# The first batch's keys and queries as fp32 loads on SyncE, with TensorE transposes and a new order of work

## The chip, the cores and the metric

The kernel runs on one NeuronCore of a Trainium2 chip. Its engines each run their own instructions in order and wait for each other through semaphores: TensorE (PE; its loads of stationary operands are listed apart as PEld), VectorE (DVE), ScalarE (ACT), GpSimd (POOL) and SyncE (SP). Loads and stores are issued by POOL, SP or ACT into DMA queues. POOL's queue (software descriptors) can change the type on the way, here fp32 to bf16; SP's and ACT's queues move plain bytes or transpose. The metric is the device time of one execution in microseconds, the median of several runs.

## What is computed

An attention over pooled keys and values, whose output goes as x into a mixture of four causal attention heads ("experts"), of which each token takes the best two. Shapes: 8 batches, 8 heads, 576 tokens, 64 per head; 512 model columns; 4 experts of width 64.

```python
k_p = k.reshape(B, H, Sp, pool, D).mean(axis=3)          # pool = 8: 72 pooled keys
v_p = v.reshape(B, H, Sp, pool, D).mean(axis=3)
scores = scale * np.matmul(q, k_p.transpose(0, 1, 3, 2))
attn = softmax(scores);  attn_out = np.matmul(attn, v_p)
x = attn_out.transpose(0, 2, 1, 3).reshape(B, S, H * D)
...
logits = x @ w_gate;  topk = 2 largest;  w = softmax over them
for e in range(E):
    q, k, v = x @ wq[e], x @ wk[e], x @ wv[e]
    a = causal softmax(scale * q @ k.T)
    out += mask[e] * w[e] * (a @ v @ wo[e])
```

## The kernel before

One long string, `SEQ` (line 606), is the whole order of work. Each token is a step, `name:batch@bank`; a trailing `d` puts a copy on VectorE instead of ScalarE, a trailing `p` keeps a store from being issued right behind its copy. The loop at line 677 emits the tokens one after the other, and TensorE, ScalarE, VectorE and POOL run their instructions in exactly that order. The order was worked out beforehand by a planner; a change of plan is a change of this string. PSUM's eight banks are given out in it by number.

The steps of a batch, in order of their data flow:

- `L_q`, `L_k`, `L_v` (`load`, line 111): POOL loads queries, keys and values and casts them to bf16 into one of three buffers each (`qraws`, `kraws`, `vraws`). A key or value block has 96 partitions of two tokens each, for all heads; three blocks (c = 0, 1, 2) make 576 tokens.
- `PK` (line 249) pools keys: the stationary operand is the small matrix `poolk` (96x32), the moving one the keys. `kc` (line 258) transposes the pooled keys in blocks of 32 on VectorE, and `kt` (line 264) copies them to bf16 (`kpTs`). `u` (`turn`, line 277) transposes the queries on VectorE from `qraws` to `qTs`.
- `E` (line 293) makes scores, `e` (line 303) their exponentials on ScalarE into `etas`: per batch four activations of 1024 columns and two of 256. `D`, `d`, `x` make the denominators and their reciprocals (a logarithm and an exponential on ScalarE), `PV`, `vc` the pooled values, `O` the outputs, and `o` (VectorE) scales them into `xTs`.
- `P`, `p` project x to expert queries and keys, `V`, `v` to values and gate, `S`, `s` make causal scores and exponentials (`etbs`), `a` masks on POOL, `B` with `bz`, `bg`, `b` multiplies by the values, `T`, `t` (or `F`, a transposing DMA on SP) transposes, `Y`, `y` applies the output weights and `z` stores.
- `g` is the gate's arithmetic; `W`, `c` load and reorder the expert weights; `H` are warm-up matmuls on a zero operand, whose results nobody reads. `I`, `J`, `K`, `M` set constants and pads.

Batch 0 is treated apart. Its keys of heads 0 to 3 do not go through POOL: `Q0` to `Q2` (`load_plain`, line 130) load them as fp32 on SP into memory that `xTs[1]` uses later, in runs of 512 bytes, and `w0` to `w2` (`cast_plain`, line 134) cast them to bf16 on ScalarE. The other heads' keys (`L_k01`, `L_k11`, `L_k21`) and the queries come through POOL. `LONG` (line 59) gives batch 0's queries another layout: each partition reads 18 tokens in a row, in two loads of long runs. `PK`, `kc` and `kt` run in two halves for it, then `u0`, `u1`, `E0` and so on. The first eighteen warm-up matmuls (`H18`) stand ahead of all that. Batches 1 to 7 share one path.

The two lines that set batch 0's SyncE loads:

```python
nc.sync.dma_start(out=plain(c).rearrange("p (h n) -> p h n", h=4),
                  in_=k[0, 0:4, 2 * KR * c : 2 * KR * (c + 1), :].rearrange("h (p t) d -> p h (t d)", t=2))
```

## Time and profile before

| | before |
|---|---|
| median of 3 runs | 158.32 us (157.78 to 158.62) |
| the profiled execution | 159.01 us |
| its span, first to last instruction | 157.3 us |
| busy: TensorE, ScalarE, VectorE, POOL | 145.2, 136.0, 122.6, 88.5 us |
| granted TensorE clock, mean | 0.996 |
| DMA, POOL's queue / SP's and ACT's | 14.92 MB / 10.82 MB |

The rows of the profile are read like this. A row of the timeline has the start, the time until its last instruction ended, engine, line of the kernel, operation, output and input names, and a count of merged instructions; in square brackets how long the engine was idle before, and for whom it waited. A row of a group has the shape, the count, the busy time and the mean duration of one in nanoseconds, and after the second bar the idle time ahead of it. The chain of waits goes back from the last instruction to what released it, step by step, so what stands in it is what set the end. A row of stretches has the busy time of each engine, the number of its instructions in brackets, then the granted clock, the DMA share and GB/s. DMA rows count packets and bytes by queue: q0 is POOL's, q1 is SP's and ACT's. All times count from the start of the span.

### The profile page before, as it was taken

What the parts mean: (1) busy time and instruction counts of PE and PEld (TensorE: products, weight loads), DVE (VectorE), ACT (ScalarE), POOL (GpSimd) and SP (SyncE); (2) the same over time, 40 slices, a digit from 0 to 9 for tenths busy, and PEclk for the clock granted to TensorE, in tenths of its full rate; (3) what the DMA queues carried; (4) which work ended last, traced back from release to release, by engine and by line L of the source; (5) the groups of instructions that cost most, each with busy time, mean ns of one, the idle gap of its engine ahead of it and who ended that gap; (6) DMA issues with size and microseconds to landing.
All of it is one profiled execution on the core that took longest, in us unless ns stands there. A gap on an engine that the chain in (4) does not pass through costs nothing.

```text
span 157.3 us, 5462 instructions
## 1 busy us (share of the span) xinstructions
PE 145.2 (92%) x2133; PEld 80.1 (51%) x2133; DVE 122.6 (78%) x404; ACT 136.0 (86%) x256; POOL 88.5 (56%) x160
## 2 busy tenths in 40 slices
PE   6939789899999999999999999999999999999960
PEld 2313235445445547546645656466375666566620
DVE  1425285679899989989989999989869599888850
ACT  4123957999999999999999999999999999999850
POOL 6867557899896989892899233223200453323200
PEclk9999999999999999999999999999999999999998
DMA  4999999999999999999999992452330371499895
GB/s 109 163 187 180 181 178 151 179 166 178 182 182 181 179 181 180 181 215 247 181 179 180 213 108 42 44 167 77 100 70 8 105 236 26 120 303 382 258 375 160
DMA packets 68602, 26.47 MB, mean 168 GB/s; under 512 B 62304, under 2 KB 63712, under 8 KB 68576
## 3 DMA queue, kind: packets, MB, share of 16 engines
q0 software_dynamic: 57008, 14.92, 94.7%
q1 hardware_dynamic: 11344, 10.82, 22.3%
q10 hardware_dynamic: 224, 0.39, 0.7%
q8 instruction: 16, 0.26, 0.6%
q14 instruction: 10, 0.08, 0.2%
HBM read 30.42 MB, written 9.44 MB: 253 GB/s over the span
## 4 chain that ended last, share of the span: by engine, by line
PE 77%; DVE 6%; ACT 6%; DMA 5%; issue 2%; SPq 1%; DVEq 0%; ACTq 0%
PE psum L205 73%; DMA xT<-in_k_dram 5%; DVE xT L360 3%; ACT eta L314 2%; PE psum L214 2%; PE psum L193 2%; ACT etb L477 2%; DVE vaug L196 1%; ACT rza L333 1%; SPq L131 1%; DVE qT L281 0%; DVE xT L351 0%; ACT rza L337 0%; ACT kraw L196 0%; DVE kf L262 0%
## 5 line engine op out<-in xcount | busy, mean ns | idle before, releaser
L477 ACT ACTIVATE etb<-psum 128x1024 bf16<-128x1024 f32 x48 | 47.4, 1036 | 0.5 <-PE psum L205 0.4
L494 POOL TENSOR_SCALAR_AFFINE_SELECT etb<-etb 128x256 bf16<-128x256 bf16 x64 | 25.7, 413 | 27.1 <-ACT etb L477 26.7
L314 ACT ACTIVATE eta<-psum 96x1024 bf16<-96x1024 f32 (+1 forms) x48 | 36.3, 811 | 3.6 <-PE psum L205 3.0
L124 POOL DMA_DIRECT2D qraw<-in_q_dram x30 | 19.8, 662 | 4.6 <-DMA vraw<-in_v_dram 2.7
L205 PEld LDWEIGHTS <-etb 128*128 128x128 bf16 x480 | 18.3, 97 | 7.5 <-issue 2.0
L360 DVE TENSOR_TENSOR xT<-psum,rza 128x512 bf16<-128x512 f32 x32 | 20.4, 683 | 2.0 <-ACT rza L337 1.1
L124 POOL DMA_DIRECT2D vraw<-in_v_dram x24 | 18.5, 772 | 5.2 <-DMA vraw<-in_v_dram 1.9
L205 PE MATMUL psum<-wvg,xT 128*128 128x260 bf16 x144 | 20.5, 275 | 0.3 <-ACT eta L314 0.3
L205 PE MATMUL psum<-wop,oT 128*128 128x512 bf16 (+1 forms) x74 | 20.4, 375 | 0.4 <-DVE oT L196 0.4
L205 PE MATMUL psum<-xT,wqp 128*128 128x512 bf16 (+1 forms) x128 | 19.8, 287 | 0.5 <-DVE xT L360 0.4
L205 PE MATMUL psum<-vaug,etb 128*128 128x65 bf16 x480 | 20.2, 194 | 0.0
L205 PE MATMUL psum<-xT,wkp 128*128 128x512 bf16 (+1 forms) x128 | 19.6, 286 | 0.1
L124 POOL DMA_DIRECT2D kraw<-in_k_dram x24 | 18.2, 761 | 1.4 <-PE psum L205 0.4
L536 DVE TENSOR_TENSOR osc<-psum,gt 128x256 bf16<-128x256 f32 (+2 forms) x40 | 16.8, 423 | 1.2
L205 PE MATMUL psum<-qk 64*128 64x64 bf16 (+4 forms) x192 | 16.4, 277 | 0.1
L205 PEld LDWEIGHTS <-xT 128*128 128x128 bf16 x144 | 12.7, 97 | 6.4 <-issue 3.0
L196 ACT COPY ofin<-psum 128x512 f32<-128x512 f32 (+1 forms) x24 | 13.4, 593 | 1.2 <-PE psum L205 0.9
L196 DVE CAST qk<-psum 128x512 bf16<-128x512 f32 (+1 forms) x21 | 13.5, 643 | 0.5 <-PE psum L205 0.4
L193 PE MATMUL psum<-warm 128*128 128x512 bf16 x43 | 12.3, 442 | 1.3 <-DVE onesd L163 1.3
L205 PE MATMUL psum<-qT,kpT 32*128 32x64 bf16 (+1 forms) x256 | 12.8, 289 | 0.7 <-DVE qT L281 0.3
L281 DVE STREAM_TRANSPOSE qT<-qraw 128x576 f32<-128x576 f32 x16 | 12.8, 817 | 0.4 <-issue 0.4
L486 POOL TENSOR_SCALAR_AFFINE_SELECT etb<-etb 64x256 bf16<-64x256 bf16 x8 | 3.4, 419 | 16.9 <-ACT etb L471 16.9
(76 smaller groups left out, 224.1 us busy)
## 6 DMA issues: line engine op xcount, KB each, us to landing
out_dram<-ofin SPq DMA_DIRECT2D x31, 256.0 KB, 3.2
vraw<-in_v_dram POOLq DMA_DIRECT2D x24, 192.0 KB, 7.2
kraw<-in_k_dram POOLq DMA_DIRECT2D x21, 192.0 KB, 7.3
qraw<-in_q_dram POOLq DMA_DIRECT2D x28, 144.0 KB, 7.6
out_dram<-ofin SPq DMA_DIRECT2D x7, 128.0 KB, 2.5
xT<-in_k_dram SPq DMA_DIRECT2D x3, 192.0 KB, 2.8
qraw<-in_q_dram POOLq DMA_DIRECT2D x2, 288.0 KB, 7.7
kraw<-in_k_dram POOLq DMA_DIRECT2D x3, 96.0 KB, 7.7
```

What stands on the lines that cost most here:

```text
L124: nc.gpsimd.dma_start(out=dst, in_=src)
L193: nc.tensor.matmul(out=psum[rows, bank, :], lhsT=warm[:, rows], rhs=warm[:], start=True, stop=True)
L196: (nc.vector.tensor_copy if dve else nc.scalar.copy)(out=out, in_=in_)
L205: nc.tensor.matmul(out=out, lhsT=lhsT, rhs=rhs, start=start, stop=stop)
L214: nc.tensor.transpose(out=out[s], in_=in_[:, s], identity=ident[0:n, 0:n])
L281: nc.vector.transpose(out=dst.rearrange("p (a s n) -> p a n s", s=32, n=n), in_=src.rearrange("p (a n d) -> p a n d", n=n, d=32))
L314: nc.scalar.activation(out=dst, in_=src, func=EXP, scale=ATT_EXP_SCALE)
L360: nc.vector.tensor_tensor(out=xT[:, 2 * got[0][0] + t : 2 * got[-1][0] + t + 1 : 2, m + got[0][1].start : m + got[0][1].stop], in0=psum[:, ...
L477: nc.scalar.activation(out=et[:, ep, :, eo : eo + n], in_=psum[:, bank : bank + 2, 0:n], func=EXP, scale=MOE_EXP_SCALE,)
L486: nc.gpsimd.affine_select(out=blk, in_=blk, pattern=[[0, NEP], [0, 2], [1, 64]], compare_op=ISGE, fill=0.0, base=0, channel_multiplier=-1,)
L494: nc.gpsimd.affine_select(out=blk, in_=blk, pattern=[[0, 2], [1, 128]], compare_op=ISGE, fill=0.0, base=0, channel_multiplier=-1,)
L536: nc.vector.tensor_tensor(out=osc(b, ep)[:, own, :].rearrange("p c (e d) -> p e c d", e=2), in0=o[:, :, :, 0:HD], in1=gt.to_broadcast([128 ...
```

## The change

Batch 0's queries and all its keys are now loaded as fp32 by SyncE, in twelve loads `Q0` to `Q11` of 192 KB each (two groups of four heads; in each group three blocks of keys, then three of queries). They lie for the time being in `xTs[1]`, `qraws[0]`, `kraws[2]` and `vraws[2]`. POOL's five loads of batch 0's queries and keys go. A new step `R6` (`pace`) is a copy on POOL that reads the last column of plain load 6; POOL's next load, of batch 0's values, stands behind it.

The keys are cast as before (`w0` to `w2` and now `w6` to `w8`; three of the six on VectorE). The pooling `PK` of batch 0 has the raw keys as stationary operand (96x64) and `poolk` as the moving one (32 columns), 48 matmuls for each group; its result is already transposed, so that `kt` is one plain copy and `kc` goes. The queries are transposed as fp32 by TensorE (`X`, four transposes a block), and `r` copies the result to bf16 on ScalarE. `N` makes scores from them, in 96x96 matmuls, and `n` their exponentials, six of 768 columns. The long query layout is removed.

The order of the whole kernel is new: `H18` is `H9`, 19 single warm-ups stand between the steps of batches 0 and 1 where 25 stood, the pads are set in three parts, some copies change between ScalarE and VectorE, and most output stores have a step of their own (`zs`) that issues them on SP later in the order.

```diff
-    def plain(c):
-        return xTs[1][0:KR].rearrange("p f n -> p (f n)").bitcast(FP32)[:, 512 * c : 512 * c + 512]
...
+    PLAIN = [(g, T, c) for g in range(2) for T in "kq" for c in range(3)]
+
+    def plain(n):
+
+        homes = [(xTs[1], 4), (qraws[0], 2), (kraws[2], 3), (vraws[2], 3)]
...
+    def load_plain(n):
+        g, T, c = PLAIN[n]
+        src = (k if T == "k" else q)[0, 4 * g : 4 * g + 4, 2 * KR * c : 2 * KR * (c + 1), :]
+        nc.sync.dma_start(out=plain(n).rearrange("p (h n) -> p h n", h=4),
+                          in_=src.rearrange("h (p t) d -> p h (t d)", t=2))
+
+    def cast_plain(n, dve):
+        g, _, c = PLAIN[n]
+        copy(dve, kraws[0][:, c, 4 * g : 4 * g + 4].rearrange("p h t d -> p (h t d)"), plain(n))
+
+    def pace(n):
+        nc.gpsimd.tensor_copy(out=mark[:], in_=plain(n)[:, 511:512])
...
+    def PK(b, bank, g=None):
         raw = kraws[b % NRAW]
+        if b == 0:
+            for c in range(3):
+                for h in range(4):
+                    for t in range(2):
+                        for u in range(2):
+                            o = KR * h + 32 * c
+                            mm(psum[64 * u : 64 * u + 64, bank, o : o + 32], raw[:, c, 4 * g + h, t, :], poolk[:, :],
+                               start=(t == 0), stop=(t == 1))
+            return
...
+    def kt(b, bank, dve, g=None):
+        if b == 0:
+            copy(dve, kp0(g), psum[:, bank, 0 : 4 * KR])
+        else:
+            copy(dve, kpTs[b % 2][:, :, 0:3].rearrange("p n c j -> p n c j"), kfs[b % 2][:])
...
+    def X0(b, bank, g, c):
+        raw = plain(6 * g + 3 + c)
+        for h in range(4):
+            nc.tensor.transpose(out=psum[:, bank, KR * h : KR * h + KR], in_=raw[:, 128 * h : 128 * h + 128],
+                                identity=ident32[:, :])
+
+    def r0(b, bank, dve, g, c):
+        copy(dve, q0(g, c), psum[:, bank, 0 : 4 * KR])
+
+    def E0(b, bank, g, c):
+        kp, qt = kp0(g), q0(g, c)
+        for h in range(4):
+            own = slice(KR * h, KR * h + KR)
+            for u in range(2):
+                rows = slice(64 * u, 64 * u + 64)
+                mm(psum[0:KR, bank + u, own], kp[rows, own], qt[rows, own])
+
+    def e0(b, bank, dve, g, c):
+        s0 = 2 * KR * c
+        dst = etas[0][:, 4 * g : 4 * g + 4, s0 : s0 + 2 * KR].rearrange("k h (p u) -> k u h p", u=2)
+        src = psum[0:KR, bank : bank + 2, 0 : 4 * KR].rearrange("k u (h p) -> k u h p", h=4)
+        nc.scalar.activation(out=dst, in_=src, func=EXP, scale=ATT_EXP_SCALE)
...
-        Q0:0 Q1:0 Q2:0 I:0 H18:0@0 L_q0:0 L_k01:0 L_k11:0 J:0 K:0 M:0 L_k21:0 L_q1:0 w0:0 L_v0:0 w1:0 w2:0 L_v1:0
-        PK0:0@0 L_v2:0 H1:0@1 H1:0@1 kc0:0 H1:0@1 H1:0@1 kt0:0 H1:0@0 H1:0@0 H1:0@0 H1:0@0 u0:0 W0:0 H1:0@0 H1:0@0
-        H1:0@0 H1:0@0 W1:0 PK1:0@0 L_k0:1 E0:0@24 kc1:0 H1:0@1 L_k1:1 kt1:0d H1:0@1 e00:0 H1:0@0 H1:0@0 H1:0@0 u1:0
-        L_k2:1 H1:0@0 e01:0 H1:0@0 L_q0:1 E2:0@02 E1:0@46 e20:0 e21:0 D0:0@0 L_q1:1 e10:0 D2:0@1 e11:0 PV:0@2 L_q2:1
...
+        I:0 J:0 K:0 Q0:0 Q1:0 Q2:0 Q3:0 Q4:0 Q5:0 Q6:0 Q7:0 Q8:0 Q9:0 Q10:0 Q11:0 H9:0@0 M0:0 w0:0d w1:0 M1:0 w2:0 M2:0
+        X00:0@0 X01:0@1 r00:0 X02:0@2 r01:0 PK0:0@0 R6:0 w6:0d L_v0:0 r02:0 H1:0@1 w7:0d H1:0@1 L_v1:0 w8:0 kt0:0d
+        PK1:0@1 L_v2:0 X10:0@0 kt1:0 W0:0 X11:0@2 r10:0 X12:0@1 W1:0 r11:0 N00:0@4 r12:0 N01:0@2 L_k0:1 n00:0 N12:0@0
+        N10:0@6 L_k1:1 n01:0 N02:0@4 L_k2:1 n02:0 N11:0@2 L_q0:1 n11:0 D0:0@4 L_q1:1 n12:0 PV:0@5 L_q2:1 H1:0@2 n10:0
...
```

More of the change, by code (lines that the diff above doesn't have):

```diff
@@ L264, in kt, with kc @@
-    def kt(b, bank, dve, j=None):
-        r = slice(2 * own(j).start, 2 * own(j).stop)
-        copy(dve, kpTs[b % 2][:, r, 0:3].rearrange("p n c j -> p c n j"), kfs[b % 2][:, :, r])
+                    mm(psum[32 * i : 32 * i + 32, bank, 128 * c : 128 * c + 128], poolk[:, :],
+                       raw[:, c, 2 * i : 2 * i + 2, t, :], start=(t == 0), stop=(t == 1))
+    def kc(b, bank, dve):
+        src = psum[:, bank, 0 : 4 * KR].rearrange("p (m s t) -> p m t s", s=32, t=2)
+        nc.vector.transpose(out=kfs[b % 2][:].rearrange("p c n j -> p (c n) j"), in_=src)
@@ L306, in es @@
         n = cols.stop - cols.start
[L307 removed]
+        by = "k (i g) s -> k i g s"
         if len(got) == 2:
```

217 lines of the change are left out of this document (110 added, 107 removed).

## The prediction

> **What bounds the kernel now.** I read the page first, then busy time by stretch.
>
> ```profile
> span 157.3 us, 5462 instructions
> 8.00:16.00 8.00, 5.62 (x75) 2.37 (x75) 3.35 (x5) 2.77 (x4) 5.50 (x8) 1.00 1.68 184
> 16.00:24.00 8.00, 6.39 (x79) 2.44 (x75) 4.31 (x10) 5.71 (x12) 4.74 (x7) 1.00 1.84 179
> 25.50:39.40 13.90, 12.96 (x181) 6.67 (x176) 11.41 (x32) 13.83 (x26) 12.71 (x21) 1.00 1.69 171
> 39.40:140.00 100.60, 100.56 (x1572) 57.71 (x1571) 90.58 (x300) 99.25 (x191) 55.47 (x105) 1.00 1.10 146
> ```
>
> Columns of a stretch: its length, then busy time of PE, PEld, DVE, ACT, POOL. From 39.4 us on TensorE has work all the time (100.56 of 100.60 us) and ScalarE nearly so (99.25). Two engines are full there, and VectorE has ten free microseconds. Before 24 us nothing is full: ScalarE has 2.77 us of work in 8 us, and much of the PE row is warm-up. The next view, the chain of waits in order of time, says why (start, length, what).
>
> ```profile
> 1.76 7.93 DMA xT<-in_k_dram
> 9.71 0.63 ACT kraw L196
> 10.38 0.24 PE psum L205 x8
> ```
>
> The third SyncE load of keys takes 7.93 us, and the cast, the pooling and the scores hang on it. Hence every later stage starts about as late as batch 0's first exponential, and this is the place where the change works. The timeline has the stage (start, length, engine, line):
>
> ```profile
> 10.98 1.21 DVE L281 STREAM_TRANSPOSE qT<-qraw 128x576 f32<-128x576 f32 x1
> 14.20 4.58 ACT L314 ACTIVATE eta<-psum 96x1024 bf16<-96x1024 f32 x6 [2.76 <-PE psum L205]
> 21.50 0.59 PE L205 MATMUL psum<-xT,wqp 128*128 128x512 bf16 x2
> ```
>
> The six exponentials start at 14.20 us and fill ScalarE for 4.58 us; the first projection follows at 21.50. My measure of the start-up is the first exponential: 14.20 before, X after.
>
> **The loads.** Three SyncE loads become twelve of 192 KB, and POOL's two query and three key loads of batch 0 go. POOL's next load stands behind R6, a copy that waits for plain load 6; behind it queue batch 0's values, the weights and all later loads, on which the pooling of values, the weight copies c and batch 1 wait.
>
> ```profile
> L131 SPq DMA_DIRECT2D xT<-in_k_dram x3: 391/463/478, 0.8 to 1.8; - x3
> DMA to landing us min/median/max: 2.7/2.8/7.9
> DMA packets 263, 0.14 MB, mean 280 GB/s; under 512 B 11, under 2 KB 257, under 8 KB 263
> q1 hardware_dynamic: 257, 0.13, 84.8%
> DMA packets 748, 0.38 MB, mean 253 GB/s; under 512 B 27, under 2 KB 742, under 8 KB 748
> DMA packets 482, 0.18 MB, mean 177 GB/s; under 512 B 370, under 2 KB 465, under 8 KB 482
> 1.32 0.70 POOL L124 DMA_DIRECT2D qraw<-in_q_dram  x1 [0.81 <-POOLq L733]
> ```
>
> The DMA answers are for 3.0 to 3.5 us (280 GB/s, 257 of 263 packets from SyncE's queue, q1), for 2.0 to 3.5 (253) and for 6 to 7 (177 GB/s, most packets under 512 B, the casting ones of POOL). So 196,608 bytes take 0.70 us at 280 and 0.78 at 253; I take 0.70, the rate with the queue full. Issuing (0.46 us each) is quicker and hides. The first load lands 2.7 us after its issue at 0.8, at 3.5; the n-th at 3.5 + 0.70n: 5.6 (first queries, n=3), 7.7 (n=6, which frees POOL), 9.1 (n=8), 11.2 (n=11). POOL's packets come late (6 of those 263, some 2 us after its first issue at 1.32), so from about 9.5 us; they slow the last two or three loads by an estimated 1 us (half of two loads' time): 12.2. POOL's own stream then carries 2.29 MB (values, two weights, batch 1's keys and queries) at 177 GB/s in 12.9 us from 10.3 us (the SyncE loads then take only the rest), to about 23.5 us; batch 1's queries are first used after 26 us:
>
> ```profile
> 26.38 1.43 DVE L281 STREAM_TRANSPOSE qT<-qraw 128x576 f32<-128x576 f32 x2
> ```
>
> So I charge nothing; the cover is about 2 us. The Trainium skill ("DMA: Bandwidth & Descriptors", section Issuing engines are not separate DMA queues) says that DMAs issued by different engines share the same 16 engines and interleave. The 7.93 us of the third load beside POOL's stream agrees, and by that rule SyncE wins nothing by itself: the gain would be the pause that R6 forces.
>
> **The work on TensorE.** Removed for batch 0: 48 pooling matmuls with one shared matrix, 48 score matmuls, two VectorE transposes of queries (1.21 us in the row above), two of pooled keys. Added: 24 fp32 transposes, 96 poolings whose stationary operand is the raw key block (96x64), 48 score matmuls of 96x96. None has its like in the trace; the nearest rows are:
>
> ```profile
> 148.50 0.22 PE L214 MATMUL psum<-ident,osc 128*128 128x128 bf16 x1
> 148.86 0.39 PE L214 MATMUL psum<-ident,osc 128*128 128x128 bf16 x4
> 59.82 1.10 PE L205 MATMUL psum<-vaug,etb 128*128 128x65 bf16 x31
> L205 PE MATMUL psum<-vaug,etb 128*128 128x65 bf16 x480 | 20.2, 194 | 0.0
> 144.08 0.45 PE L205 MATMUL psum<-qk 64*128 64x64 bf16 x8
> L205 PEld LDWEIGHTS <-etb 128*128 128x128 bf16 x480 | 18.3, 97 | 7.5 <-issue 2.0 <-POOL etb L494 0.4 <-POOL etb L486 0.4
> ```
>
> Four bf16 transposes take 0.39 us where one takes 0.22, so 0.057 us each. For fp32 the bounds are the same, 0.057, and four passes, 0.23; I take twice, 0.11, as the bytes double: 0.46 us per group of four (0.23 to 0.92). Pairs of load and small matmul come 0.030 us apart (31 in 1.10 us, less the 0.19 of the last one) and 0.037 (8 in 0.45, less 0.19, over 7); one 128-column load by itself takes 0.097. I take 0.037, since that stationary operand also fills half an array side: 48 poolings are 1.8 us (1.4 to 4.7). The Trainium skill ("TensorEngine Tiling (Array Packing)", Restrictions) says that column tiling switches off the fast weight load, which the 64-wide blocks would meet; its page "TensorE: Matmul & The Clock Gate" (LDWEIGHTS) has columns / 1.2 ns, an estimate of 53 ns or 2.6 us for 48. No run here shows such a load; by it X would be 1.6 us later.
>
> In TensorE's order: transposes X00 5.6 to 6.1, X01 6.3 to 6.8, X02 7.0 to 7.5; PK0 7.5 to 9.3. PK1 waits for the last key cast:
>
> ```profile
> L196 ACT CAST kraw<-xT x3: 616/617/618, 3.5 to 9.7; 96x512 bf16<-96x512 f32 x3
> ```
>
> 9.1 + 0.62 = 9.75; PK1 to 11.55, X10 12.0, X11 12.5, X12 13.0 (its load at 12.2). Then ScalarE copies X12's block, 128x384, and the first exponential stands behind that:
>
> ```profile
> L196 ACT CAST qk<-psum 128x512 bf16<-128x512 f32 x14 | 8.3, 594 | 2.4 <-PE psum L205 2.4
> L314 ACT ACTIVATE eta<-psum 96x256 bf16<-96x256 f32 x16 | 5.4, 378 | 0.4
> L314 ACT ACTIVATE eta<-psum 96x1024 bf16<-96x1024 f32 x32 | 30.9, 1027 | 3.2 <-PE psum L205 3.0
> ```
>
> About 0.5 us (a quarter less than 594 ns): X = 13.0 + 0.1 + 0.5 = **13.6**. The scores N00 (8 pairs, 0.3 us) run under that copy. The exponentials cover the same 4,608 columns in six equal pieces instead of four of 1024 and two of 256, so I keep 4.58 us. The casts w6 and w7 and the copy kt0 fall into VectorE's idle time (3.35 us of work between 8 and 16 us; without it each would add some 0.6 us). Batch 2's keys and values go into the homes of plain loads 6 to 11, which are read out by 13 us, and are issued long after: nothing. The start-up gives **-0.6 us**, with X from 12.5 (all low ends, no contention) to 21 (poolings at 0.097 us, transposes at 0.23); at 0.78 us a load it would be 14.2, no gain.
>
> **The replanned rest.** Matmuls, exponentials and masks after batch 0 are the same. By the letters in the order, ScalarE gives up 1 projection copy of 512 columns and 2 of 256, 3 pooled-value copies and 5 output copies, and takes 3 value copies with their gate column, 5 transposed-output copies of 256 less one of 64, and 2 pooled-key copies:
>
> ```profile
> L196 ACT COPY ofin<-psum 128x512 f32<-128x512 f32 x23 | 13.0, 603 | 0.6 <-PE psum L205 0.4
> L196 ACT CAST vaug<-psum 128x256 bf16<-128x256 f32 x15 | 5.7, 386 | 0.0
> L196 ACT COPY L<-psum 128x4 f32<-128x4 f32 x15 | 2.8, 188 | 0.0
> L196 ACT CAST qk<-psum 128x256 bf16<-128x256 f32 x5 | 2.0, 395 | 0.0
> L196 ACT CAST vp<-psum 96x512 bf16<-96x512 f32 x3 | 1.8, 592 | 0.0
> L196 ACT COPY oT<-psum 128x256 bf16<-128x256 bf16 x4 | 1.6, 392 | 0.2 <-PE psum L214 0.2
> L196 ACT COPY oT<-psum 128x64 bf16<-128x64 bf16 x2 | 0.4, 216 | 0.0
> L196 ACT CAST kpT<-kf 128x384 bf16<-128x384 f32 x1 | 0.5, 511 | 0.0
> ```
>
> 0.59 + 0.79 + 1.78 + 3.02 less 1.72 + 1.96 - 0.22 + 1.02 is 6.18 - 4.48 = 1.7 us off ScalarE, and some 3 us more on VectorE, hidden in its 10 free microseconds after 39.4 (if they were gone, +3). As TensorE is full beside ScalarE, I count a third, **-0.6 us** (0 to -1.7). The issue of output stores moves to tokens of its own on SyncE, whose queue has nothing else late but the transposing copies: nothing.
>
> **The sum.** The profiled execution took 159.01 us, 1.7 more than its span, 0.7 above the median 158.32. 159.01 - 1.2 = 157.8 for such an execution, **157.1** on the median; with the ends above other than the slow ones, 154.9 to 158.3.
>
> **The rivals.**
> A, slower: TensorE becomes the bound of the start-up. The place is PK0 to X12; transposes at 0.92 us a group and poolings at 2.3 us (half of 97 ns per 64 columns). X00 ends 6.5, X01 7.4, X02 8.4, PK0 10.7, PK1 13.0, X12 15.7, X 16.4, or +2.2, less 0.6 of relief: **159.9**. It decides once two poolings and six groups of transposes pass about 7.5 us (my terms give 6.4; at 2.1 and 0.55 us X is 14.1). For it: a 128-column load by itself lasts 0.097 us, and nothing in the trace has a new 64-column operand for each matmul. Against it: in the rows above such loads overlap the matmuls before them. The tiling page's rule, by which the poolings take 2.6 us (its estimate above), speaks for this rival.
>
> B, slower: the clock. In the start-up, warm-up matmuls come some 0.4 us apart, then 0.20 (6 in 1.18):
>
> ```profile
> 1.26 6.25 PE L193 MATMUL psum<-warm 128*128 128x512 bf16 x18 [1.26 <-DVE onesd L163]
> 5.50 0.15 PEld L193 LDWEIGHTS <-warm 128*128 128x128 bf16 x1 [0.28 <-issue]
> 5.84 1.18 PEld L193 LDWEIGHTS <-warm 128*128 128x128 bf16 x6 [0.18 <-issue]
> ```
>
> About eleven fill 1.26 to 5.84 (0.42 each); the speed-up comes 4.5 us after the first. H9 instead of H18 ends at 1.26 + 9 x 0.42 = 5.0. If PE stays at half rate until PK0 is done (transposes 0.92, PK0 3.6): 12.0, PK1 13.8, X12 15.2, X 15.8: +1.6 - 0.6, **159.3**. The Trainium skill ("TensorE: Matmul & The Clock Gate", Part 1) ties the release to a free-running window of about 3.4 us; the rows agree with one such window, and whether 3.9 us of warm-up suffice would then vary.
>
> C, faster: everything at its low end: X 12.5, relief 1.7: 158.3 - 3.4 = **154.9**. Against it: contention at 9 to 12 us.
>
> D, nothing: TensorE's 100.56 us stay and batch 1's loads, paused by R6, eat the 0.6 us at the start: **158.2**.
>
> **How the numbers follow.** The forecast 45%, A 22%, B 12%, C 13%, D 8%. A measurement of this kernel can tell about 0.5%, 0.8 us. Of the forecast's 45 points 36 lie beyond that and 9 within; C's 13 are faster, D's 8 within; of A's 22 and B's 12 four lie within and 30 are slower. Faster 36 + 13, same 9 + 8 + 4, slower 30. The range reaches from C's 154.9 to 160.4, past A's 159.9; above it lies only the part of A with loads near 0.097 us. The forecast alone: 156.0 to 158.2.
>
> **What would show it.** Plain load 11 landing near 12 us; four transposes in about 0.5 us; 48 poolings in about 1.8; first eta activation near 13.6 and first projection near 20.9; ScalarE about 1.7 us less busy after that. A first exponential after 15 us speaks for A or B (B if warm-up matmuls of 512 columns are still 0.42 us apart). I am wrong if X comes at 13.6 and the end does not move.

## The result and the profile after

| | before | changed |
|---|---|---|
| median | 158.22 us (157.78 to 158.62, 4 runs) | 165.7 us (163.63 to 168.95, 4 runs) |
| ratio to before | | 1.0386, 95% interval 1.0297 to 1.0475 |
| profiled execution, span | 159.01, 157.3 us | 168.95, 167.2 us |
| granted TensorE clock, mean | 0.996 | 0.933 |
| busy: TensorE, ScalarE, VectorE | 145.2, 136.0, 122.6 us | 152.0, 139.8, 125.0 us |

The change is slower, where 157.1 was forecast. The medians are over all four executions, the ratio is of those within 1.5% of their kernel's fastest (163.63 and 165.02 us of the changed kernel), and the profiled execution is the longest, so its stretches show where the time went better than how much. A line of the changed kernel's page (the granted clock in 40 equal slices of the span, in tenths of full speed), and its busy time by stretch (columns as in the prediction):

```profile
PEclk9955559999999999999999999978999999999997
```

```profile
8.00:16.00 8.00, 7.78 (x123) 6.13 (x124) 1.68 (x3) 3.56 (x8) 6.02 (x8) 0.52 1.27 179
16.00:24.00 8.00, 7.22 (x101) 3.64 (x103) 1.26 (x4) 7.71 (x11) 5.08 (x8) 0.50 1.71 166
42.00:150.00 108.00, 103.59 (x1605) 60.25 (x1594) 94.78 (x299) 100.50 (x195) 56.61 (x107) 0.98 1.05 141
```

Two things are new. First, TensorE's granted clock, 1.00 in the rows of before, is 0.52 and 0.50 from 8 to 24 us, and in the same stretches TensorE, which had free time before (5.62 and 6.39 us), is nearly full (7.78 and 7.22). Second, the late stretch has gaps: TensorE is idle for 4.4 of 108 us, where before it was idle for 0.04 of 100.6. The start in the timeline (start, length, engine, line):

```profile
1.26 3.88 PE L208 MATMUL psum<-warm 128*128 128x512 bf16 x9 [1.26 <-DVE onesd L176]
7.52 0.53 PE L296 MATMUL psum<-ident,xT 96*128 96x96 f32 x4 [2.38 <-DMA xT<-in_q_dram]
9.95 1.46 PE L220 MATMUL psum<-poolk,kraw 96*64 96x32 bf16 x48
11.63 0.62 ACT L211 CAST kraw<-kraw 96x512 bf16<-96x512 f32 x1 [1.09 <-DMA kraw<-in_k_dram]
12.31 1.46 PE L220 MATMUL psum<-poolk,kraw 96*64 96x32 bf16 x48
16.42 5.38 ACT L314 ACTIVATE eta<-psum 96x768 bf16<-96x768 f32 x6
24.59 2.68 PE L208 MATMUL psum<-warm 128*128 128x512 bf16 x10
27.11 1.03 PE L220 MATMUL psum<-xT,wqp 128*128 128x512 bf16 x4
```

The first exponential, 14.20 before, starts at 16.42, and the first projection, 21.50 before, at 27.11. So 2.2 us are lost before the exponentials and 3.4 behind them: 0.8 because they last 5.38 us instead of 4.58, the rest in denominators, outputs and ten warm-up matmuls (2.68 us) that stand in TensorE's order ahead of the projection. The late gaps, in the view of TensorE's waits (total, times, longest) and in the chain of waits in order of time:

```profile
PE psum L220 <- DMA oT<-osc: 3.4, 2, 1.7
```

```profile
105.00 4.35 DMA oT<-osc
144.17 3.95 DMA oT<-osc
```

`oT<-osc` are the transposing transfers that SyncE issues for the output. Twice TensorE stands for 1.7 us in front of an output step `Y` whose transfer has not landed. In the timeline SyncE issues these transfers one after the other:

```profile
105.00 1.26 SPq L611 DMA_TRANSPOSE oT<-osc  x1
```

### The profile page after: what moved, and what is told of

It is laid out like the page before. It is cut to its first block, busy times and chain, and to the rows that moved or that the text cites. A ratio compares the mean times of both kernels' runs of the same rounds, so it can differ in the third digit from the quotient of the medians.

```text
span 167.2 us, 5623 instructions
## 1 busy us (share of the span) xinstructions
PE 152.0 (91%) x2206; PEld 87.6 (52%) x2206; DVE 125.0 (75%) x403; ACT 139.8 (84%) x263; POOL 85.6 (51%) x156
## 4 chain that ended last, share of the span: by engine, by line
PE 72%; DVE 9%; DMA 8%; ACT 3%; issue 3%; SPq 1%; DVEq 0%
PE psum L220 65%; DMA oT<-osc 5%; DMA qraw<-in_q_dram 3%; PE psum L208 3%; PE psum L296 2%; DVE qT L328 2%; ACT eta L314 2%; PE psum L229 2%; DVE qk L211 2%; DVE xT L407 1%; SPq L140 1%; DVE ofin L211 1%; DVE wvg L211 1%; DVE kf L276 1%; ACT etb L524 1%
## 5 line engine op out<-in xcount | busy, mean ns | idle before, releaser
L361 ACT ACTIVATE eta<-psum 96x1024 bf16<-96x1024 f32 (+1 forms) x42 | 31.5, 813 | 2.1 <-PE psum L220 1.7
L220 PE MATMUL psum<-wvg,xT 128*128 128x260 bf16 x144 | 21.3, 279 | 1.4 <-DVE wvg L211 0.8
L121 POOL DMA_DIRECT2D qraw<-in_q_dram x28 | 18.5, 664 | 1.2 <-DMA wst_q<-in_moe_wq_dram 0.8
L121 POOL DMA_DIRECT2D kraw<-in_k_dram x21 | 16.1, 776 | 0.7 <-PE psum L220 0.4
L211 DVE CAST qk<-psum 128x512 bf16<-128x512 f32 (+1 forms) x24 | 15.0, 625 | 1.7 <-PE psum L220 1.3
L220 PE MATMUL psum<-qk 64*128 64x64 bf16 (+4 forms) x192 | 15.5, 277 | 0.6 <-DVE xT L407 0.4
L211 DVE COPY ofin<-psum 128x512 f32<-128x512 f32 (+1 forms) x18 | 12.0, 673 | 5.0 <-PE psum L220 2.5
L220 PE MATMUL psum<-eta,vp 96*32 96x512 bf16 (+1 forms) x256 | 13.9, 312 | 0.0
L211 ACT COPY ofin<-psum 128x512 f32<-128x512 f32 (+1 forms) x19 | 10.7, 585 | 3.5 <-PE psum L220 3.3
L384 ACT ACTIVATE rza<-rza 128x512 f32<-128x512 f32 (+1 forms) x24 | 12.5, 528 | 0.4
```

What stands on the lines that cost most here:

```text
L121: nc.gpsimd.dma_start(out=dst, in_=src)
L211: (nc.vector.tensor_copy if dve else nc.scalar.copy)(out=out, in_=in_)
L220: nc.tensor.matmul(out=out, lhsT=lhsT, rhs=rhs, start=start, stop=stop)
L361: nc.scalar.activation(out=dst, in_=src, func=EXP, scale=ATT_EXP_SCALE)
L384: nc.scalar.activation(out=rz, in_=rz, func=EXP, scale=-1.0)
```

## The experiments

Each was run beside before on the same chip; the ratio to before is given with its 95% interval. The kernels of different parts ran on different chips (parts 1 to 6 on one), so ratios are the safer comparison between them.

### 1. Eighteen warm-up matmuls again

```diff
-  Q10:0 Q11:0 H9:0@0 M0:0
+  Q10:0 Q11:0 H18:0@0 M0:0
```

> The changed kernel with eighteen warm-up matmuls at the start instead of nine, nothing else. Theory 1 (half clock in the start-up): the first transposes wait for their load until 7.5 us anyway, so the nine more are hidden; the granted clock stays at 1.0 from 6 us on, the six transposed blocks and the two poolings run at full rate, the first exponential comes at 14.5 to 15 us instead of 16.4, the first projection at 23 to 24 instead of 27.1, and the time falls from 165.7 to about 162 with a spread under 1.5 us. Theory 2 (the new order of the later batches): the time stays at 164.5 or more, because the waits for the transposing DMA at 107 and 146 us remain. Theory 3 (the loads): the first exponential stays at 16 us because the last load sets it.

Measured: 164.8 us, ratio 1.0431 (1.0326 to 1.0537). The timeline:

```profile
9.74 0.94 PE L220 MATMUL psum<-poolk,kraw 96*64 96x32 bf16 x48
11.47 1.53 PE L220 MATMUL psum<-poolk,kraw 96*64 96x32 bf16 x48
```

The same 48 poolings take 0.94 us in the first half and 1.53 in the second: the clock is full until about 11 us and then falls all the same. The first exponential starts at 15.65 us and the projection at 26.26, and the ratio is no better than the changed kernel's. So the first theory did not come true as it was put: the number of warm-ups at the start is not the cause by itself.

### 2. The front alone, and the new order alone

The first has the changed kernel's order up to the last of batch 0's exponentials and before's order behind; the second has before's order up to that point and the changed order behind.

> The changed kernel's first 70 steps (its loads, poolings, transposes, scores and exponentials of batch 0, with nine warm-ups), followed by the order of the kernel before for everything else. Theory 2 (later order) expects the waits for the transposing DMA to vanish (under 0.6 us in all, as before) and the time to fall by 3 to 4 us against the changed kernel, to about 162. Theory 1 and 3 (start-up) expect the start-up to remain late by 2 to 5 us and so about 161 to 163 as well, but with TensorE's clock at half until 20 us and with the spread of the changed kernel; if the start-up is the whole cause, it stays at 165.

> The kernel before up to its last exponential of batch 0 (its loads through POOL, its poolings, its eighteen warm-ups), followed by the changed kernel's order for everything else. Theory 2 (later order) expects most of the loss here: 161 to 163 us, with the two waits for the transposing DMA of about 1.7 and 2 us. Theory 1 and 3 expect about 158.3, as before.

Measured: the front alone 163.36 us, ratio 1.0356 (1.0271 to 1.0441); the order alone 159.17 us, 1.0071 (1.0028 to 1.0114). By the ratios about 5.6 us of the loss belong to the front and 1.1 to the order, which the second theory had at 161 to 163 us by itself. In the second, the relief of ScalarE that the forecast counted on is small: 135.2 us busy against 136.0.

### 3. The two late output steps moved

```diff
-  Y1:2@3 ... E2:6@04 O11:6@7 y1:2dp
+  S12:4@0 Y1:2@4 s12:4 y1:2dp
...
-  s03:6 Y4:5@2 a01:7
+  Y0:5@0 Y4:5@4 y2:5p
```

Both `Y` that waited are put later in TensorE's order (with their copies and stores, and in a free bank); nothing else changes.

> The changed kernel with two steps of the output projection moved later in TensorE's order (the first chunk of batch 2 by some 30 steps, the tail chunk of batches 4 and 5 by some 25), each with its copy and store. Theory 2 expects the two waits of TensorE for the transposing DMA (1.7 us at 107, about 1.7 at 146) to shrink below 0.8 us each and the time to fall by 2 to 3 us, to about 163. The rival, that these waits are only where a delay made elsewhere shows (ScalarE full), expects the time within 1 us of 165.7.

Measured: 163.16 us, ratio 1.0328 (1.0251 to 1.0405). That is 2.5 us below the changed kernel by the medians, but 0.9 by the ratios, whose intervals overlap widely. Stretches, changed kernel first, then this one:

```profile
100.00:120.00 20.00, 18.34 (x264) 10.42 (x265) 15.81 (x46) 16.88 (x34) 3.65 (x10) 0.91 0.32 90
140.00:150.00 10.00, 8.27 (x105) 4.78 (x102) 7.55 (x28) 7.44 (x14) 3.17 (x8) 1.00 0.44 123
```

```profile
100.00:120.00 20.00, 19.76 (x273) 10.65 (x270) 18.16 (x55) 18.90 (x36) 4.42 (x11) 1.00 0.44 123
140.00:150.00 10.00, 9.56 (x128) 5.75 (x127) 8.55 (x29) 9.04 (x19) 3.53 (x9) 1.00 0.78 265
```

TensorE has 1.4 and 1.3 us more work in the two stretches, and the waits for `oT<-osc` are gone: that these steps were the waits is shown. What the waits cost is less sure than the 2.7 us of the two stretches say, since the changed kernel's row is from its longest execution; with the same late order the waits are 2.1 us in part 1 and 3.0 in part 5. One more thing stands in this profile: nothing was changed in its start, and yet the first exponential comes at 14.55 us (16.42) and the projection at 24.85 (27.11), because the loads landed earlier in this execution.

### 4. TensorE's waits filled with warm-up matmuls

```diff
-  H9:0@0 ... X00:0@0 X01:0@1 r00:0 X02:0@2
+  H22:0@0 ... X00:0@0 H2:0@3 X01:0@1 r00:0 H2:0@3 X02:0@2
...
-  kt0:0d PK1:0@1 L_v2:0 X10:0@0 kt1:0 W0:0 X11:0@2
+  kt0:0d H1:0@3 PK1:0@1 L_v2:0 X10:0@0 kt1:0 W0:0 H1:0@3 X11:0@2
```

The two single warm-ups ahead of the second pooling become pairs too.

> The changed kernel with 22 warm-up matmuls for its 9 at the start and 8 more set between the transposes, the poolings and the first scores (they stand in TensorE's waits for loads); nothing else is moved. Theory 'half clock': the start is late since TensorE's clock is halved while it waits for loads between 7 and 11.5 us, and 18 warm-ups end too early (6.6 us) to prevent it; with the waits filled the clock stays at 1.0 past 12 us, the 48 poolings of the second half take 0.94 us (1.46 to 1.53 so far), the 12 transposes under 1.6 us (2.18), the first exponential starts at 13.9 to 14.5 us (16.4, 15.65 with 18 warm-ups), the first projection at 22 to 24 us (27.1, 26.3), and the time is 161 to 162.5 us (165.7). Rival 'loads': the last key's cast ends at 12.3 us whatever the clock, and the exponentials' 5.4 us follow it anyway: first exponential not before 15.3 us, time 164 to 165.5. Rival 'order': the clock halves in spite of the fillers, since transposes and poolings keep TensorE busy but not with streaming; then durations stay at 1.5 and 2.18 us and the fillers cost up to 0.8 us: 165 to 166.5.

Measured: 162.36 us, ratio 1.0255 (1.0206 to 1.0304), though it does more. That is 3.3 us below the changed kernel by the medians and 2.1 by the ratios, and 2.4 below the kernel of part 1, whose interval lies wholly above this one. Timeline, then stretches:

```profile
10.55 0.62 ACT L211 CAST kraw<-kraw 96x512 bf16<-96x512 f32 x1 [0.65 <-DMA kraw<-in_k_dram]
11.37 0.94 PE L220 MATMUL psum<-poolk,kraw 96*64 96x32 bf16 x48
14.12 5.39 ACT L314 ACTIVATE eta<-psum 96x768 bf16<-96x768 f32 x6
25.45 1.03 PE L220 MATMUL psum<-xT,wqp 128*128 128x512 bf16 x4
```

```profile
8.00:16.00 8.00, 7.22 (x166) 5.42 (x165) 1.66 (x3) 5.53 (x11) 7.12 (x10) 1.00 1.49 194
16.00:24.00 8.00, 7.10 (x70) 2.88 (x70) 3.90 (x9) 6.31 (x11) 5.74 (x9) 0.60 1.80 179
```

With the waits filled the clock is 1.00 from 8 to 16 us, and the first exponential starts at 14.12, 2.3 us earlier than in the changed kernel. Not all of that is the clock. From the start of the second pooling to the first exponential it is 2.75 us here and 4.11 in the changed kernel (4.18 in part 1, 4.10 in part 3): 1.4 us for the half clock. The other 0.9 us is loads that landed earlier in this execution (the last key's cast begins at 10.55, not 11.63), as they did in part 3 without any filling. But TensorE is sparse again from 15 to 19.5 us, behind the exponentials, the clock falls there (0.60), and the projection comes at 25.45, not at 22 to 24. Against part 1's profile the span is 2.2 us shorter (161.1 and 163.3): 0.8 up to the projection (25.45 and 26.26), with loads that landed 1.2 us earlier too, and 1.1 in the waits for `oT<-osc`, which shrink from 2.1 to 1.0. So the clock is shown as a cause; its share of the whole gain is not.

### 5. Four of the plain loads issued by ScalarE

```diff
-        nc.sync.dma_start(out=plain(n)...
+        (nc.scalar if n in (1, 3, 5, 7) else nc.sync).dma_start(out=plain(n)...
```

> The changed kernel with four of its twelve plain loads (numbers 1, 3, 5, 7) issued by ScalarE in place of SyncE. Theory 'queue': one queue moves 231 to 241 GB/s and holds the loads at 0.85 us each; with two the rate is 270 GB/s or more between 6 and 10 us, the seventh load lands under 9.2 us (9.98) and the second at or under 5 us (the next cast after the first at 4.4 us starts at 6.56 in the changed kernel): 1 to 2 us off the time if nothing else holds. Theory 'engines': the 16 DMA engines are the limit at 512-byte pieces, and the rate stays within 5% of 235 GB/s: casts where they were to 0.4 us, time within 1 us of 165.7 (the issues on ScalarE may delay its casts by some tenths).

Measured: 164.81 us, ratio 1.034 (1.0227 to 1.0453). Stretches of the changed kernel, then of this one; the last column is GB/s:

```profile
6.00:7.00 1.00, 0.00 (x0) 0.00 (x0) 0.00 (x0) 0.44 (x1) 0.00 (x0) 1.00 1.22 241
8.00:9.00 1.00, 0.78 (x5) 0.61 (x4) 0.00 (x0) 0.48 (x1) 0.00 (x0) 0.64 1.24 234
```

```profile
6.00:7.00 1.00, 0.19 (x2) 0.22 (x3) 0.00 (x0) 0.60 (x1) 0.00 (x0) 1.00 1.20 265
8.00:9.00 1.00, 0.89 (x7) 0.88 (x8) 0.00 (x0) 0.30 (x1) 0.00 (x0) 0.77 1.24 241
```

A second queue brings 10% at most and within a microsecond of time nothing: the queue is not what holds the loads. What does (the size of their 512-byte pieces, or the memory behind) was not taken apart.

### 6. Scores of the first half earlier, then the later output steps too

On top of the filled waits, `N00` to `N02` and their exponentials stand ahead of the second pooling, and that half's copies are on VectorE; then the two moved output steps are added, with five instead of ten warm-ups before the projection.

> The kernel with filled waits, and in addition the three score groups of the first four heads and their exponentials set ahead of the second half's pooling and transposes (their operands are there at about 11 us), the second half's copies from PSUM on VectorE. Theory 'order': the changed kernel starves ScalarE between 7 and 15.7 us (busy 0.2 to 0.6 of each microsecond) although three of its six exponentials could run there: first exponential at 11.3 to 12.2 us, last one ends at 17 to 18.5 us (21.8), and if the clock holds the first projection starts at 21.5 to 23 us: 159.5 to 161.5 us, 1 to 2 below the kernel with filled waits alone. Rival 'values': what D and O need next is the value loads, which start at 10 us and end near 18.5 us, so that exponentials that end earlier gain nothing behind them: last exponential early, projection still 24 us or later, time within 0.7 us of the kernel with filled waits.

> The kernel with early scores, with the two groups of output work that wait for transposing transfers set later in TensorE's order as in the earlier run on that alone, and 5 instead of 10 single warm-ups ahead of the first projection. If the parts add up (crossbar waits 2 to 2.5 us, five warm-ups 1.05 us at full clock of which TensorE waits at least half for the normalised outputs anyway): 2.5 to 3 us below the kernel with early scores, 156.5 to 159 us. If the waits for transposing transfers come back in another place (the order behind is otherwise the same, but 4 us earlier): less than 1 us below it.

Measured: 162.15 us, ratio 1.0196 (1.0113 to 1.0279), and 161.54 us, 1.0223 (1.0173 to 1.0274). The timeline of the first:

```profile
12.22 2.79 ACT L314 ACTIVATE eta<-psum 96x768 bf16<-96x768 f32 x3 [1.50 <-PE psum L220]
18.36 0.61 PE L220 MATMUL psum<-vraw,poolv 96*32 96x512 bf16 x6 [1.02 <-ACT eta L314]
24.77 1.03 PE L220 MATMUL psum<-xT,wqp 128*128 128x512 bf16 x4
```

The exponentials start 1.9 us earlier than with filled waits alone, and the projection gains 0.7. The pooling of the values starts at 18.36, which I took for the values' late transfer. The row itself names another cause, an exponential, and part 8 shows it to be right. The parts didn't add up: the moved output steps and five warm-ups less gave 0.6 us by the medians where 2.5 to 3 was the first expectation, and nothing by the ratios. With other timing the waits for transfers had already shrunk from 3.4 to 1.5 us.

### 7. When POOL is let go, and before's order behind

```diff
-  PK0:0@0 R6:0 w6:0d L_v0:0
+  PK0:0@0 R3:0 w6:0d L_v0:0
```

The first run has this and three more warm-ups before the pooling of the values; the second puts before's order behind its front; the third has no `R` at all.

> The best version so far (early scores, filled waits, later output work) with GpSimd's stream let go by the fourth plain load instead of the seventh, and 3 more warm-ups ahead of the pooling of the values. Theory 'values': what sets the first projection there is the values' transfers, which GpSimd issues from 9.48 us on (before: 4.89) and which let the pooling of the values start at 17.80 (before: 17.03); let go at about 7 us, they start 2.0 to 2.5 us sooner, the pooling of the values at 16 to 17 us, the first projection at 21.5 to 22.3 (23.13), the time 1 to 1.5 us lower (161.5). Rival 'one pool of bandwidth': the values' transfers take from the plain loads what they gain; the second half's keys and queries land 1.5 to 2 us later, the last exponential ends at 19.5 us or later (17.6), and the time stays within 0.7 us.

> The front of the run with the earlier release of GpSimd, and behind it the order of before in place of the changed kernel's. If the replanned order behind costs something by itself when its two waits for transposing transfers are taken out (it cost 1.1 us with them, behind the old front), this is up to 0.7 us faster than the same front with the changed order; if those waits were all of its cost, the two are equal to 0.5 us. Denominators of the tails stand ahead of the pooling of the values here, so that TensorE is held there until the sixth exponential: some tenths against it.

> The same as the run with the earlier release, with no holding back of GpSimd at all: values and weights are issued from about 1 us on, beside the twelve plain loads. By the step of the forecast that laid the late third load of before on GpSimd's stream, the plain loads slow to 1.2 to 1.4 us each, the last lands at 15 to 17 us, the first half's exponentials move from 11.7 to 13 us or later, the second half's end at 20 to 21 us: 1 to 3 us slower than with the release at the fourth load. Rival: the sum of bytes is what counts, and the values come early enough to make up for it: within 0.7 us of it.

Measured: 160.52 us, ratio 1.0123 (1.0048 to 1.0199); 161.82 us, 1.0221 (1.0164 to 1.0279); 167.55 us, 1.0576 (1.0511 to 1.064). TensorE of the third:

```profile
20.13 0.90 PE L296 MATMUL psum<-ident,vraw 96*128 96x96 f32 x4 [0.26 <-DMA vraw<-in_q_dram]
29.40 0.93 PE L220 MATMUL psum<-xT,wqp 128*128 128x512 bf16 x3
```

Without the pause the last plain load holds TensorE at 20.1 us and the projection starts at 29.40: holding POOL back is worth 7.0 us to this front, more than twice what was expected. The clock is part of it: it is at 0.50 there from 14 to 26 us. Letting it go at the fourth load in place of the seventh does no harm. The second run's projection came at 23.60 at half clock, so it tells nothing of the order behind.

### 8. The pooling of the values

First without the three extra warm-ups, and with three instead of five ahead of the projection; then with the five kept and the extra ones cut to two, and the pooling in another PSUM bank, with POOL let go by the fourth and by the seventh load.

```diff
-  N12:0@4 ... PV:0@5
+  N12:0@4 ... PV:0@7
```

> The version with the earlier release of GpSimd, without the three warm-ups ahead of the pooling of the values and with three instead of five ahead of the first projection. If TensorE's own order holds the pooling of the values there (18.52 us, while the third value transfer has landed by about 17.0), it starts at 17.5 us, the first outputs at 18.8 to 19.2 (20.03), the first projection at 21.2 to 21.8 (22.49), and the time is 159.0 to 159.8 us, still at or above before's 158.0 to 158.4. If the warm-ups held the clock rather than TensorE, it falls to half between 18 and 22 us, the outputs take 2.2 instead of 1.3 us, and the time is 160.5 to 161.5.

> The version with GpSimd let go by the fourth load, the pooling of the values put into another PSUM bank (7 for 5), and two instead of three warm-ups ahead of it. In the runs with early scores the last scores stand in banks 4 and 5, so the pooling of the values may have waited for the exponential that reads them (18.16 to 18.32 us there, the pooling at 17.8 to 18.5), not for the values. Theory 'bank': the pooling starts at 17.4 to 17.8 us with the clock still full, the first projection at 21.3 to 22 us, time 159 to 160 us. Theory 'values': the pooling stays at 17.8 us or later whatever the bank: 160.3 to 161.3 us. Either way it is not expected below before.

> The same with GpSimd let go by the seventh load, as in the changed kernel. Theory 'bank': the wait was the exponential alone, so this is equal to the run with the earlier release to 0.5 us. Theory 'values': the pooling starts 0.7 us or more later than there (values issued 1.5 to 2 us later), the first projection too, and the time is 0.7 to 1.5 us above it.

Measured: 161.22 us, ratio 1.0202 (1.0139 to 1.0264); 160.0 us, 1.0097 (1.0057 to 1.0138); 160.59 us, 1.0128 (1.0092 to 1.0165). The first run in the timeline:

```profile
17.78 0.74 PE L220 MATMUL psum<-vraw,poolv 96*32 96x512 bf16 x6 [1.02 <-ACT eta L314]
18.85 1.06 PE L208 MATMUL psum<-warm 128*128 128x512 bf16 x2 [0.33 <-issue]
```

Without the warm-ups TensorE waits 1.02 us for the exponential that reads the shared bank, and then two warm-ups take 1.06 us, where two take 0.60 in part 4 at full clock: the clock has gone again, as the second expectation had it. With the other bank the wait is gone, and the runs with early and with late values agree: the pooling starts at 18.52 and 18.46 us, the projection at 22.50 and 22.44. So neither expectation came true to the letter: the bank was the wait, the values were not, and what then set both was a late start (first exponential at 12.92 and 12.87, where the first run of part 7 has 12.38 and the same projection, 22.49). That the bank was the wait shows best in the first run of part 9, where the pooling begins at 17.13 us, before the last exponential ends at 17.65. The 22 warm-ups ended at 9.04 us there and held up the first transposes; in part 4 the same 22 ended at 7.52. The rows, the run with the early release first:

```profile
1.26 7.78 PE L208 MATMUL psum<-warm 128*128 128x512 bf16 x22 [1.26 <-DVE onesd L176]
```

```profile
1.26 6.26 PE L208 MATMUL psum<-warm 128*128 128x512 bf16 x22 [1.26 <-DVE onesd L176]
```

### 9. What is left

```diff
-  H22:0@0
+  H19:0@0
...
-  n11:0 L_q0:1
+  n11:0 W2:0 W3:0 L_q0:1
```

The first run adds this to the other bank and the early release; the second puts before's order behind its first projections.

> The version with the other bank and the earlier release, with 19 instead of 22 warm-ups at the start (in its profile the 22nd ended after the fourth load had landed, and the first transposes came late, at about 8.9 us) and the value and gate weights issued on GpSimd ahead of the next batch's queries instead of behind them (TensorE waits 0.8 us for their reordered copy between 30 and 40 us, 0 in before). If the two are what is left: first exponential 12 to 12.4 us (12.9), first projection 21.6 to 22.1 (22.5), the wait for the value weights gone, 158.4 to 159.3 us, equal to before within its scatter. If the queries of the next batch now come late instead (a wait for them of 0.5 us or more at 28 to 32 us) or the clock halves again: 159.7 us or more.

> The front of the run with 19 warm-ups (its first projection starts at 21.1 us, before's at 21.5, and TensorE's waits between 30 and 40 us are gone) through the first projections, and behind it the order of before. Theory 'order behind': what is left of the loss there (1.7%, with TensorE idle 1.4 us more than before between 60 and 150 us) is the replanned order, so this comes to 157.6 to 158.8 us, equal to before or up to half a microsecond below it. Rival 'front': something of the new front still costs later (transfers of the next batches in another order): 159.5 us or more.

Measured: 160.25 us, ratio 1.0166 (1.0099 to 1.0233), and 159.82 us, 1.0126 (1.0075 to 1.0177). The first run's timeline:

```profile
11.54 2.79 ACT L314 ACTIVATE eta<-psum 96x768 bf16<-96x768 f32 x3 [1.50 <-PE psum L220]
21.12 0.93 PE L220 MATMUL psum<-xT,wqp 128*128 128x512 bf16 x3
```

In this execution the front is as early as before's: projection at 21.12 (21.50), the gate's first step at 33.18 (33.27), and the clock is whole. Its span is nevertheless 158.4 us against 157.3. From 60 to 150 us, before's row, this one's, and that of the second run, which has before's order there:

```profile
60.00:150.00 90.00, 89.93 (x1409) 53.50 (x1406) 80.20 (x272) 88.53 (x175) 40.17 (x83) 1.00 0.93 158
```

```profile
60.00:150.00 90.00, 88.49 (x1376) 52.23 (x1373) 81.59 (x267) 85.95 (x170) 39.93 (x82) 1.00 0.92 157
```

```profile
60.00:150.00 90.00, 88.73 (x1395) 53.51 (x1406) 80.28 (x270) 88.62 (x175) 41.38 (x84) 1.00 0.93 154
```

TensorE is idle for 1.51 us there, 0.07 before. The theory that the new order behind is what is left did not come true: with before's order TensorE is still idle for 1.27 us, and the time is 159.82, as the rival 'front' said. One part of that rival shows on VectorE in the second run:

```profile
28.34 1.44 DVE L328 STREAM_TRANSPOSE qT<-qraw 128x576 f32<-128x576 f32 x2 [1.50 <-DMA qraw<-in_q_dram]
```

The turning of batch 1's queries, at 26.38 us before, waits 1.50 us for their loads; in the first run it waits 0.83 us, as its expectation had feared. In part 8, where the value and gate weights still stand behind these queries on POOL, it does not wait. So this wait came with the moved weights. What the rest of the loss is stays open, and no version beats before.

## Why the prediction was wrong

**The start-up's sum (the step that failed).** The forecast gave the start-up -0.6 us; in the profile the first projection is 5.6 us later than before. The sum's own steps, beside three kernels (us; part 3's has the changed kernel's start unaltered):

| | forecast | changed | part 3 | part 4 |
|---|---|---|---|---|
| last key's cast begins | 9.1 | 11.63 | 10.15 | 10.55 |
| second pooling begins | 9.75 | 12.31 | 10.45 | 11.37 |
| first exponential | 13.6 | 16.42 | 14.55 | 14.12 |
| first projection | 20.9 | 27.11 | 24.85 | 25.45 |

Two terms failed. The loads came later than 0.70 us apiece: the last key's cast is 2.5 us late, of the 2.8 by which the first exponential missed, and in part 3's execution 1.0 us late. And the clock was taken as full, from the transposes on and in the 7.3 us that were carried over to the projection. It does not show between the second pooling and the first exponential (forecast 3.85 us, measured 4.11), by luck: there the poolings were priced too high, and at full clock it is 2.75 (part 4).

**The clock.** Half rate was rival B, at 12% and 159.3 us, ending with the first pooling. In the profile it lasts from 8 to 25 us, so it also slows the second pooling, the later transposes, scores, denominators and outputs. B had the right mechanism, its end was wrong, and so was its cause: it blamed `H9`, and with `H18` the clock fell too. TensorE mostly waits for loads between 5 and 8 us, and warm-ups in the waits held the clock (part 4), which is 1.4 us up to the first exponential. Behind it the profiles don't give the clock's share, as the clock fell again there. Whether the waits take the clock away, or the kind of work between them, was not separated. In the changed kernel TensorE is busy without a gap from 9 to 17 us, with transposes, poolings, two warm-ups and scores, and the clock stays at half:

```profile
9.00:17.00 8.00, 8.00 (x146) 6.52 (x146) 1.68 (x3) 4.07 (x8) 7.02 (x10) 0.50 1.31 168
```

One of the changed kernel's executions has a mean granted clock of 1.00 and takes 165.02 us all the same. It left no trace, and the record can miss a fall (last section), so it does not decide against the clock. The Trainium skill ("TensorE: Matmul & The Clock Gate", Part 1) lets the gate close after an idle window of about 3.4 us. In part 1 it closed at about 11 us although the longest wait ahead of it was 1.05 us, while before has a wait of 2.64 us without loss. That does not refute the page: from 6.61 to 10.60 us TensorE did only transposes and poolings in part 1, and no run here shows whether these count as idle. The two waits, part 1 first:

```profile
7.67 0.52 PE L296 MATMUL psum<-ident,xT 96*128 96x96 f32 x4 [1.05 <-DMA xT<-in_q_dram]
```

```profile
10.38 0.24 PE L205 MATMUL psum<-kraw,poolk 96*32 96x64 bf16 x8 [2.64 <-ACT kraw L196]
```

**The loads.** I took 0.70 us a load, at 280 GB/s; between 6 and 11 us the changed kernel's loads move at 235:

```profile
DMA packets 2394, 1.18 MB, mean 235 GB/s; under 512 B 96, under 2 KB 2394, under 8 KB 2394
```

That is 0.84 us each. The row of 3.0 to 3.5 us that I used was half a microsecond near the start, not the rate over several loads. The third load is late again, though POOL issues its first load only at 10.35 us; so POOL's stream was not the whole cause of the 7.93 us. The cast behind the third load and POOL's first loads, in the timeline:

```profile
6.56 0.62 ACT L211 CAST kraw<-xT 96x512 bf16<-96x512 f32 x1 [1.62 <-DMA xT<-in_k_dram]
10.35 2.43 POOL L121 DMA_DIRECT2D vraw<-in_v_dram  x3
```

The forecast had that load landed at 4.9 us (3.5 + 2 x 0.70); why it is late is open. From its cast at 6.56 to the last key's at 11.63, six loads are 0.85 us apart. The forecast's own "14.2, no gain" at 0.78 us a load is near the 14.12 that part 4 has with the clock cured, by luck: its loads are later still, its poolings shorter. The sentence that SyncE wins nothing but the pause that `R6` forces agrees with part 7: without the pause the same front loses 7.0 us. The Trainium skill ("DMA: Bandwidth & Descriptors", section Issuing engines are not separate DMA queues) states that engines' transfers share one set of DMA engines, and part 5 agrees (234 and 241 GB/s with one and two issuers).

**TensorE's sizes (rival A).** Four transposes, forecast 0.46 us, took 0.53; 48 poolings, forecast 1.8, took 1.46 at half clock and 0.94 at full. A falls: both are under its 0.92 and 2.3 us, even at half clock for the poolings.

**The exponentials.** I kept 4.58 us because the columns are the same. They took 5.38: a piece of 768 columns has a mean of 1027 ns, as long as one of 1024 (1027 ns in the prediction's row); why is open:

```profile
L314 ACT ACTIVATE eta<-psum 96x768 bf16<-96x768 f32 x6 | 5.4, 1027 | 0.0
```

**Hidden work between exponentials and projection.** I carried the 7.3 us between the two over unchanged (20.9 after 13.6). They became 10.7: 0.8 for the longer exponentials, the rest at half rate and with ten warm-ups ahead of the projection, where before has five. The two were not taken apart.

**The replanned rest.** Forecast -0.6 us from 1.7 us less work on ScalarE; alone it costs 1.1 us and takes 0.8 us from ScalarE. The cost that I set at "nothing", with SyncE's queue as its cover, is there: twice TensorE waits for the transposing transfers, 3.4 us in the profile, and moving the two steps brings 0.9 us by the ratios and 2.5 by the medians. Of batch 1's loads I said that 2 us of cover hide them, and that held: their turning does not wait in the changed kernel, nor in the last run of part 8, with `R6` and the projection at 22.44; the waits of part 9 came with the moved weights.

**How it adds up.** By medians: filled waits 3.3 us, then early scores 0.2, later output steps and fewer warm-ups 0.6, POOL's earlier release and warm-ups that hold the clock 1.0, the other bank 0.5; 160.0 remains against 158.6, of which the new order alone would explain 1.1. By ratios the chain is 1.0386, 1.0255, 1.0196, 1.0223, 1.0123, 1.0097. The intervals of neighbours overlap at each step; clear of the scatter (1 to 2 us between executions) are only the fall over the whole chain and that from part 1 to part 4.

## What to carry to other kernels

A stage in which TensorE waits for loads can pay twice, when the clock falls as well: ask of every change to a start-up what TensorE will be doing in each of its microseconds, and read the granted clock by stretches, not only the mean. Take a transfer's rate from a stretch of its steady state. Before a gain in a start-up is put down to an edit, look how much the same start varies by itself: here its first exponential came at 16.42 and at 14.55 us with no edit to it. And a step that is moved nearer to the transfer it consumes needs the transfer's own chain priced (here 1.2 us an issue and 4 us to landing), even where the queue looked idle before.

## What the hardware showed that I had not expected

The clock record can miss a change. In the run with the front alone the stretches give the full clock from 2 to 20 us, but the same 48 poolings take as long as at half clock elsewhere:

```profile
12.00:13.00 1.00, 1.00 (x46) 1.00 (x42) 0.00 (x0) 0.00 (x0) 1.00 (x2) 1.00 1.62 159
```

```profile
11.72 1.46 PE L220 MATMUL psum<-poolk,kraw 96*64 96x32 bf16 x48
```

The duration of a known instruction is the better clock. At full clock a pooling with its own 64-column stationary operand costs 0.020 us (0.94 over 48), under the 0.030 us that the nearest row of before gave. And two things vary by themselves and move everything behind them: the cast behind the third plain load begins at 5.20 us in the first run of part 9 and at 6.77 in part 1, with the same loads ahead; and 22 warm-ups at the start take 6.26 or 7.78 us (part 8), as the clock rises sooner or later. The loads of their stationary operand come 0.43 us apart until 4.12 us in part 4 and until 7.15 us in part 8, and about 0.2 apart from then on:

```profile
4.12 2.90 PEld L208 LDWEIGHTS <-warm 128*128 128x128 bf16 x14 [0.17 <-issue]
```

```profile
7.15 1.39 PEld L208 LDWEIGHTS <-warm 128*128 128x128 bf16 x7 [0.22 <-issue]
```

The Trainium skill ("TensorE: Matmul & The Clock Gate", Part 1) has the gate decide by a free-running window of about 3.4 us, and this spread of 3.0 us, less than one window, agrees with it.
